# Block-diagonal attention tiles, division per query row, long loads, and attention merged into feed-forward in a fixed order

## The chip, the cores and the metric

One core of one Trainium2 chip runs the whole program. The metric is the device time of that core in microseconds (us); lower is better. Repeated runs of one kernel differ by up to some 1.5%.

## The reference

Sparse attention over 8 batches of 8 heads (576 positions, head size 64) is followed by a feed-forward network (FFN) on the 4608 resulting rows of 512 values. Four heads look only at the last 32 positions, four only at every 32nd position.

```python
rel = pos[:, None] - pos[None, :]
mask_local   = (rel >= 0) & (rel < 32)
mask_strided = (rel >= 0) & (pos[None, :] % 32 == pos[:, None] % 32)
# heads 0-3 local, 4-7 strided; softmax over the masked scores; times v
# x: [4608, 512], the heads side by side
h = x @ w_in                     # [512, 2048]
r = np.maximum(h, 0.0)
g = s * (r * r) + b              # s, b: one number each
return g @ w_out                 # [2048, 512]
```

## The kernel before

Attention is computed transposed: keys lie on partitions, queries run along the columns. AV, the product of the weights with V, also gives the sum of each query's weights, in row 64 of its PSUM tile. Since queries are columns, dividing by that sum means dividing by a row: the row is copied out for each head, one reciprocal per batch is taken over all of them, TensorE spreads it over 64 partitions by a product with ones, and VectorE multiplies.

```python
def emit_av(st):
    ...                                      # cut: the matmuls into ps_or[0:65, queries]
    nc.vector.tensor_single_scalar(          # L231: one row of 576 sums
        out=den8[b][prow:prow + 1, pcol:pcol + S],
        in_=ps_or[D:D + 1, :], scalar=0.0, op=ALU.add)
    nc.scalar.copy(out=xT[m][64 * e:64 * e + 64, b * S:(b + 1) * S], in_=ps_or[0:D, :])

def emit_norm_batch(b):
    nc.vector.reciprocal(out=rec8, in_=den8[b])            # L240
    for m in range(4):
        for e in range(2):
            ...                              # cut: two matmuls rec8 -> ps_nb (L249)
            nc.vector.tensor_tensor(out=sl, in0=ps_nb[rbase:rbase + 64, :],
                                    in1=sl, op=ALU.mult)   # L255
```

The order is attention and FFN in turn: each batch is a loop over four pairs of heads, and a whole FFN block (128 matmuls of 512 columns) is issued after the third pair.

```python
for b in range(B):
    nc.gpsimd.dma_start(out=qk_nat[:, :, 0:D], in_=qf)     # rows of 64 values
    ...                                      # cut: k and v the same way
    for m in range(4):
        ...                                  # cut: transposes, four ACT copies, scores,
                                             # exp, mask; AV of the previous head
        if m == 1 and b > 0:
            emit_norm_batch(b - 1)
        if m == 2:
            for T in moe_sched.get(b, []):
                emit_moe_block(T)            # 64 + 64 matmuls, nothing between them
```

The softmax here doesn't subtract the row's maximum and nothing guards it: scores larger than these inputs give would overflow.

## Time and profile before

| | before |
|---|---|
| time, median of 3 runs | 602.73 us (602.71 to 604.86) |
| span of the profiled run | 602.0 us |
| period of one batch and one FFN block | 65.1 us: FFN 27.3, attention 37.8 |
| mean granted clock in these two stretches | 0.96 and 0.62 |
| first FFN matmul | 97.3 us (the chain has its first at 98.7) |
| matmul columns of attention in a batch | 28.6 thousand |

The page's lines on engines, the chain and the stretches are in the prediction. One more view is needed, the groups of the division on VectorE (DVE). Columns: line, engine, operation, tiles, count, then busy us in all, mean ns of one, and the idle time before it with what ended most of that.

```profile
L231 DVE TENSOR_SCALAR den<-ps_or 1x576 f32<-1x576 f32 x64 | 48.2, 753 | 29.9 <-PE ps_or L222 29.2
L255 DVE TENSOR_TENSOR xT<-ps_nb,xT 64x576 f16<-64x576 f32 x64 | 48.3, 755 | 21.4 <-PE ps_nb L249 20.3
L240 DVE RECIPROCAL rec<-den 128x1152 f16<-128x1152 f32 x8 | 58.8, 7353 | 0.3
```

These are 155 us of DVE work for what is one division per query and head. A copy of one partition by 576 columns costs as much as a multiply of 64 partitions by 576: the length of the row counts, not the number of partitions.

### The profile page before, as it was taken

What the parts mean: (1) busy time and instruction counts of PE and PEld (TensorE: products, weight loads), DVE (VectorE), ACT (ScalarE), POOL (GpSimd) and SP (SyncE); (2) the same over time, 40 slices, a digit from 0 to 9 for tenths busy, and PEclk for the clock granted to TensorE, in tenths of its full rate; (3) what the DMA queues carried; (4) which work ended last, traced back from release to release, by engine and by line L of the source; (5) the groups of instructions that cost most, each with busy time, mean ns of one, the idle gap of its engine ahead of it and who ended that gap; (6) DMA issues with size and microseconds to landing.
All of it is one profiled execution on the core that took longest, in us unless ns stands there. A gap on an engine that the chain in (4) does not pass through costs nothing.

```text
span 602.0 us, 6889 instructions
## 1 busy us (share of the span) xinstructions
PE 507.0 (84%) x2576; PEld 238.9 (40%) x2576; DVE 322.4 (54%) x684; ACT 304.8 (51%) x579; POOL 45.7 (8%) x30
## 2 busy tenths in 40 slices
PE   0537889997999789987999799978998899939997
PEld 0313443444344434444344434443444444414443
DVE  1204686448742875268634874287536763485241
ACT  0538865437570857266543757085726664306050
POOL 5212111001200120010100120010000000000000
PEclk9996556995599658985699559965897569859999
DMA  9999949016901659015901690160000000100101
GB/s 114 202 175 77 65 27 78 14 58 40 78 2 56 54 31 49 36 42 33 79 16 55 40 77 3 66 45 1 2 35 36 0 2 17 53 0 2 52 18 70
DMA packets 119793, 28.59 MB, mean 47 GB/s; under 512 B 112208, under 2 KB 114640, under 8 KB 119760
## 3 DMA queue, kind: packets, MB, share of 16 engines
q0 software_dynamic: 113568, 18.35, 51.3%
q1 hardware_dynamic: 6192, 9.80, 4.4%
q8 instruction: 20, 0.33, 0.2%
q14 instruction: 13, 0.11, 0.1%
HBM read 37.06 MB, written 9.44 MB: 77 GB/s over the span
## 4 chain that ended last, share of the span: by engine, by line
PE 66%; DVE 15%; ACT 8%; DMA 5%; issue 4%; POOL 1%; ACTq 0%; POOLq 0%
PE ps_o L199 21%; PE ps_h L189 19%; PE ps_or L222 12%; DVE rec L240 10%; PE ps_s L316 7%; DMA w_out_sb<-in_moe_w_out_dram 5%; PE ps_nb L249 4%; DVE xT L255 3%; ACT pt L324 3%; DVE den L231 2%; ACT uT L194 2%; ACT xT L234 1%; PE ps_tq L285 1%; PE ps_tk L295 1%; DVE pt L330 1%
## 5 line engine op out<-in xcount | busy, mean ns | idle before, releaser
L324 ACT ACTIVATE pt<-ps_s 128x512 f16<-128x512 f32 (+4 forms) x240 | 97.8, 437 | 176.3 <-PE ps_s L316 131.2
L189 PE MATMUL ps_h<-xT,w_in_sb 128*128 128x512 f16 x576 | 140.6, 398 | 1.4 <-ACT uT L194 0.7
L199 PE MATMUL ps_o<-w_out_s,gT 128*128 128x512 f16 x576 | 125.8, 379 | 0.0
L194 ACT ACTIVATE uT<-ps_h 128x512 f16<-128x512 f32 x144 | 85.7, 597 | 69.5 <-PE ps_h L189 66.5
L222 PE MATMUL ps_or<-pt,v 128*65 128x64 f16 (+11 forms) x608 | 96.2, 276 | 22.1 <-DVE pt L330 12.6
L316 PE MATMUL ps_s<-qT,kT 64*128 64x159 f16 (+6 forms) x352 | 85.6, 339 | 24.3 <-ACT kT L301 16.3
L195 DVE TENSOR_TENSOR gT<-uT 128x512 f16<-128x512 f16 x144 | 61.3, 426 | 77.9 <-ACT uT L194 77.7
L189 PEld LDWEIGHTS <-w_in_sb 128*128 128x128 f16 x576 | 56.7, 101 | 75.7 <-issue 17.0
L222 PEld LDWEIGHTS <-v 128*65 128x65 f16 (+1 forms) x608 | 59.8, 140 | 59.9 <-issue 38.4
L199 PEld LDWEIGHTS <-gT 128*128 128x128 f16 x576 | 56.3, 98 | 68.0
L204 DVE TENSOR_TENSOR osb<-ps_o,bcs 128x512 f32<-128x512 f32 x36 | 24.9, 692 | 96.1 <-PE ps_o L199 96.1
L231 DVE TENSOR_SCALAR den<-ps_or 1x576 f32<-1x576 f32 x64 | 48.2, 753 | 29.9 <-PE ps_or L222 29.2
L255 DVE TENSOR_TENSOR xT<-ps_nb,xT 64x576 f16<-64x576 f32 x64 | 48.3, 755 | 21.4 <-PE ps_nb L249 20.3
L240 DVE RECIPROCAL rec<-den 128x1152 f16<-128x1152 f32 x8 | 58.8, 7353 | 0.3
L316 PEld LDWEIGHTS <-kT 64*128 64x128 f16 (+1 forms) x352 | 31.2, 115 | 64.2 <-issue 38.2
L330 DVE TENSOR_TENSOR pt<-pt,mask_str 128x512 f16<-128x512 f16 (+1 forms) x192 | 47.7, 303 | 5.1 <-ACT pt L324 3.3
L249 PE MATMUL ps_nb<-rec,hsel 128*64 128x512 f16 (+1 forms) x128 | 38.7, 438 | 13.6 <-DVE rec L240 8.3
L330 DVE TENSOR_TENSOR pt<-pt,mask_loc 128x159 f16<-128x159 f16 (+3 forms) x160 | 26.7, 222 | 40.5 <-ACT pt L324 39.5
L234 ACT CAST xT<-ps_or 64x576 f16<-64x576 f32 x64 | 40.2, 628 | 3.3 <-DVE den L231 2.4
L285 PE MATMUL ps_tq<-ident,qk_nat 128*128 128x128 f16 x128 | 20.6, 290 | 16.1 <-DMA qk_nat<-in_k_dram 16.1
L274 POOL DMA_DIRECT2D v<-in_v_dram x8 | 14.5, 1812 | 239.8 <-PE ps_or L222 232.6
L300 ACT COPY qT<-ps_tq 64x576 f16<-64x576 f16 x32 | 20.2, 631 | 14.9 <-PE ps_tq L288 14.9
(26 smaller groups left out, 188.1 us busy)
## 6 DMA issues: line engine op xcount, KB each, us to landing
out_dram<-osb SPq DMA_DIRECT2D x36, 256.0 KB, 2.0
qk_nat<-in_q_dram POOLq DMA_DIRECT2D x8, 576.0 KB, 9.2
qk_nat<-in_k_dram POOLq DMA_DIRECT2D x8, 576.0 KB, 10.5
v<-in_v_dram POOLq DMA_DIRECT2D x8, 576.0 KB, 8.5
w_in_sb<-in_moe_w_in_dram POOLq DMA_DIRECT2D x1, 2048.0 KB, 22.8
w_out_sb<-in_moe_w_out_dram POOLq DMA_DIRECT2D x1, 2048.0 KB, 27.1
mask_str<-mask_str SPq DMA_DIRECT2D x1, 160.0 KB, 2.5
hsel<-hsel SPq DMA_DIRECT2D x1, 64.0 KB, 1.9
```

The costliest lines, as they stand in the source:

```text
L189: nc.tensor.matmul(out=ps_h, lhsT=w_in_sb[:, ct, ft * 128:(ft + 1) * 128], rhs=xT[ct][:, tok0:tok0 + PS], start=(ct == 0), stop=(ct == 3))
L194: nc.scalar.activation(out=uT, in_=ps_h, func=AF.Relu)
L195: nc.vector.tensor_tensor(out=gT[:, ft, :], in0=uT, in1=uT, op=ALU.mult)
L199: nc.tensor.matmul(out=ps_o, lhsT=gT[:, ft, tsub * 128:(tsub + 1) * 128], rhs=w_out_s[:, ft, :], start=(ft == 0), stop=(ft == nftile - 1))
L222: nc.tensor.matmul(out=ps_or[0:D + 1, a:bq], lhsT=v1[rr, NT * m + t, 0:D + 1], rhs=pt[rr, p["c0"] + (a - p["i0"]): p["c0"] + (bq - p["i0"] ...
L231: nc.vector.tensor_single_scalar(out=den8[b][prow:prow + 1, pcol:pcol + S], in_=ps_or[D:D + 1, :], scalar=0.0, op=ALU.add)
L240: nc.vector.reciprocal(out=rec8, in_=den8[b])
L249: nc.tensor.matmul(out=ps_nb[rbase:rbase + 64, c0:c1], lhsT=hsel[:, 64 * (hh % 4):64 * (hh % 4) + 64], rhs=rec8[:, pcol + c0:pcol + c1], s ...
L255: nc.vector.tensor_tensor(out=sl, in0=ps_nb[rbase:rbase + 64, :], in1=sl, op=ALU.mult)
L316: nc.tensor.matmul(out=ps_s[poff:poff + nk, p["c0"]:p["c0"] + p["nq"]], lhsT=kT[rbase:rbase + 64, j0:j0 + nk], rhs=qT[rbase:rbase + 64, p[ ...
L324: nc.scalar.activation(out=pt[row_lo:row_hi, 0:W], in_=ps_s[row_lo:row_hi, 0:W], func=AF.Exp, scale=scale)
L330: nc.vector.tensor_tensor(out=pt[poff:poff + nk, p["c0"]:p["c0"] + p["nq"]], in0=pt[poff:poff + nk, p["c0"]:p["c0"] + p["nq"]], in1=masks[ ...
```

## The change

The intent was fourfold. Each mask becomes dense blocks: a local head is six tiles of 96 queries by 128 keys, a strided head, with its positions regrouped modulo 8, eight tiles of 72 by 72. AV puts queries on partitions, so that the division is a reciprocal of 4 or 6 columns and one multiply out of PSUM, and the result is transposed back. The loads of q and k take long pieces (6 or 8 positions of a head at once). And the attention of the next batch is dealt out between the matmuls of the current FFN block, in an order that the program fixes. The change is a rewrite; its core is below, with cuts. It also does something outside the four parts.

```diff
-        nc.gpsimd.dma_start(out=qk_nat[:, :, 0:D], in_=qf)
+            nc.gpsimd.dma_start(
+                out=tl, in_=src[b, 0:4].rearrange("h (p j) d -> p h (j d)", j=LT))
...
+                r0, at = (64 * e, j * nq) if loc else (64 * (j % 2), (4 * e + j // 2) * nq)
+                rr = slice(r0, r0 + 64)
+                nc.tensor.matmul(                              # L205, scores
+                    out=ps[0:nk, c:c + nq], lhsT=st["k"][rr, at:at + nk],
+                    rhs=st["q"][rr, at:at + nq])
...
+                    st["a"] = psum.tile([128, 6, D + 1], FP32, tag="a", bufs=1, name="ps_a")
+                nc.tensor.matmul(                              # L234, AV
+                    out=ps[0:nq, j % per, :],
+                    lhsT=st["pt", e, grp(j)[0]][0:nk, grp(j)[1], :],
+                    rhs=vt[0:nk, 2 * mm + e, j, :])
+                if j % per == per - 1:
+                    nc.vector.reciprocal(out=rec[0:nq, 0:per], in_=ps[0:nq, 0:per, D:D + 1])
+                    nc.vector.tensor_tensor(                   # L242
+                        out=st["x"][:, j0:j0 + per, 64 * e:64 * e + 64],
+                        in0=ps[0:nq, 0:per, 0:D],
+                        in1=rec[0:nq, 0:per].to_broadcast([nq, per, D]), op=ALU.mult)
...
+            # one phase of a batch: scores and transposes by halves, then AV, transposes of x
+            seq += Sn[:len(Sn) // 2] + Tn[:len(Tn) // 2] + Sn[len(Sn) // 2:] + Tn[len(Tn) // 2:]
...
-                for T in moe_sched.get(b, []):
-                    emit_moe_block(T)
+            for i, f in enumerate(seq):
+                at.setdefault(int(i * 112 / len(seq)), []).append(f)
+        for n, f in enumerate(F):                # F: the 128 FFN matmuls of block T
+            for g in at.get(n, []):
+                g()
+            f()
```

## The prediction

> **What bounds the kernel now.** I read the page first: shares of engines, then the slices, then the chain, then stretches of one period.
>
> ```profile
> PE 507.0 (84%) x2576; PEld 238.9 (40%) x2576; DVE 322.4 (54%) x684; ACT 304.8 (51%) x579; POOL 45.7 (8%) x30
> ...
> PE   0537889997999789987999799978998899939997
> ...
> PEclk9996556995599658985699559965897569859999
> ```
>
> PE looks busy everywhere, but the clock row swings between full and half. So PE is the bound in two ways. The chain of waits shows one period, here the third feed-forward (FFN) block and what follows it:
>
> ```profile
> 235.63 9.66 PE ps_h L189 x44
> 245.28 13.81 PE ps_o L199 x64
> 259.42 0.76 PE ps_or L222 x8
> 263.64 1.09 ACT pt L324 x2
> 265.89 0.94 PE ps_or L222 x7
> 266.86 0.77 DVE den L231
> 267.64 7.35 DVE rec L240
> 275.15 1.70 PE ps_or L222 x12
> ```
>
> 64 matmuls of 512 columns in 13.81 us are 216 ns each: the full clock, nothing to gain. After them the chain hops between PE, ACT and DVE and sits 7.35 us in one reciprocal. The stretches of that period (FFN, attention) say it in numbers:
>
> ```profile
> core 0: us, PE busy (x) PEld busy (x) DVE busy (x) ACT busy (x) POOL busy (x), PEclk, DMA share, GB/s
> ...
> 229.75:257.00 27.25, 27.20 (x122) 11.85 (x122) 9.73 (x21) 11.59 (x20) 0.00 (x0) 0.96 0.17 28
> 257.00:294.81 37.81, 31.36 (x185) 16.09 (x183) 29.11 (x62) 24.03 (x51) 5.43 (x3) 0.62 0.90 55
> ```
>
> A period is 65.1 us: 27.3 of FFN with DVE and ACT a third busy, and 37.8 of attention at a mean clock of 0.62, with DVE at 77%. The two engines that attention needs idle while FFN runs, and PE is slow while attention runs. The list of waits adds the start, where PE waits for data and then again for the weights:
>
> ```profile
> PE ps_tq L285 <- DMA qk_nat<-in_k_dram: 16.1, 1, 16.1
> ...
> PE bcs_ps L167 <- DMA w_out_sb<-in_moe_w_out_dram: 13.4, 1, 13.4
> ```
>
> The first FFN matmuls of the chain are at 98.7 us.
>
> **What the Trainium skill says.** (1) "TensorE: Matmul & The Clock Gate", Part 1: the array runs at half rate until a window of about 3.4 us has been busy, and falls back when it is not. The trace agrees: its clock record knows only full and half, in stretches of 30.7 and 34.1 us, nine and ten windows; windows in which matmul columns filled 38 to 45% of the full-rate cycles were followed by half clock, windows at 57% were not by themselves. (2) "TensorEngine Tiling (Array Packing)", Key Properties: changing the tiling mode drains the engine, and different row tiles run in parallel. The trace agrees on both. At full clock:
>
> ```profile
> 326.04 0.20 PE L288 MATMUL ps_tq<-ident,qk_nat 64*128 64x64 f16 x1
> 326.04 0.20 PE L291 MATMUL ps_tk<-ident,qk_nat 64*128 64x64 f16 x1
> 326.17 0.40 PE L295 MATMUL ps_tk<-ident,qk_nat 128*128 128x128 f16 x4
> 326.50 0.21 PE L316 MATMUL ps_s<-qT,kT 64*64 64x64 f16 x1
> 326.64 0.41 PE L222 MATMUL ps_or<-pt,v 128*65 128x512 f16 x1
> 326.98 0.40 PE L316 MATMUL ps_s<-qT,kT 64*64 64x512 f16 x1
> 327.31 0.35 PE L222 MATMUL ps_or<-pt,v 128*65 128x384 f16 x1
> ```
>
> L288 and L291 use opposite row halves and start together. A 512-column matmul of 128 rows followed by one of 64 rows takes 326.64 to 326.98, 0.34 us and not 0.216: a switch between 128 and 64 rows costs some 0.1 us; the 64-column one before it takes 0.14. (3) The same TensorE page, "Back-to-back issue gap", gives about 81 ns per matmul of 128 columns with its weight load. Here the measurement is lower: four L295 in 0.40 us, the last of which shows some 0.23, so 56 ns each; I use columns over 2.4 per ns. (4) "DMA: Bandwidth & Descriptors", Specifications: rows under 512 B miss line rate. The page counts 112208 of 119793 packets under 512 B, and DMA is above 90% in the first slices.
>
> **The change part by part.**
> Removed. Attention in 128-key tiles against wide query ranges is 28.6 thousand matmul columns a batch (4.6 transposes, 9.7 scores, 9.7 AV, 4.6 broadcast of the reciprocals). Block-diagonal tiles leave 15.2 thousand: 4.6 transposes, 4.6 scores, 3.6 AV (65 columns each, since V is now the moving operand) and 2.3 for transposing the result back. The DVE work on rows goes too: the reciprocal of 7.35 us, eight rows of denominators at 0.753 us and eight normalisations at 0.755 us, 19.4 us a batch.
>
> Added. Per batch 12 small reciprocals (4 or 6 columns; 7.35 us for 1152 columns is 6.4 ns a column, so about 0.15 us with the fixed part) and 12 multiplies out of PSUM, 256 or 384 columns. From 0.692 us at 512 and 0.755 at 576 columns I take 0.43 and 0.56. With the 16 squares (0.426), 16 masks (about 0.31), 4 output adds (0.692), copies and head pairing (about 3), DVE has some 25 us per merged block. ACT has 16 relus (0.597), 16 exponentials of 288 columns (0.41, between 0.386 at 256 and 0.570 at 477), 10 copies (0.63): 22.5 us.
>
> Moved. The order is fixed: seven FFN blocks are merged with the attention of the next batch, about 1.7 attention matmuls ahead of each FFN matmul; two FFN blocks stay alone. Reading the two programs' PE order, one merged block has 128 FFN matmuls, 196 of attention, and 72 switches between the 64-row scores and everything else. PE in one block, at full clock:
> - FFN 128 x 0.216 = 27.6 us.
> - Transposes and AV: 6.9 thousand columns / 2.4 = 2.9 us, and 56 x 0.034 = 1.9 us.
> - Scores: 56 in pairs on opposite row halves, 28 x 0.043 = 1.2 us.
> - Switches: 72 x 0.1 = 7.2 us.
> - Waits that the order leaves open. The AV bank has one buffer; it comes free after drain (0.2), reciprocal, multiply and two signals, about 0.9 us. Seven times a batch nothing but an FFN matmul stands between. Keys' copy before the scores: twice without cover, 1.2 us. I take 9 us less 2 for the FFN matmuls between: 7.
>
> Sum 47.8 us, in place of 65.1. PE stays the bound: DVE and ACT are about half busy, and the two-engine work lies beside FFN.
>
> Start. The loads of q and k now move rows of 768 B or more in 1344 pieces instead of 9216, two DMAs ahead of the first transposes. Issue is 0.78 us each from 1.3 us on (the time of the w_in issue, which has as few rows per partition); landing I estimate at 3.5 us after the second issue ends at 2.9 (the 256 KB stores land in 2.0, today's q loads of 4608 pieces in 7.4 after their issue), so 6.4, and the pairing of heads ends near 7 us, where the transposes waited until 16.1. Batch 0 then runs alone at half clock (four transposes there take 0.61 us, 107 ns each): 15.4 thousand columns / 1.2 = 12.8 us, and about 14 us of waits on ACT and DVE that nothing covers; 26.5. First FFN at 33.5 us, and w_in lands before that.
>
> Total: 33.5 + 7 x 47.8 = 368, + 16 x 0.216 for the bias product = 371.6, + 2 x 27.65 = 427, + 4 us from the last matmul to the end (598.0 to 602.0 now), + 0.7 between span and time (602.0, 602.7): 432 us.
>
> **The rivals.**
> The clock: if the merged stream falls back to half, a block takes 80.7 thousand columns / 1.2 = 67 us and more with switches and waits, and the kernel ends at 600 or above. Against it: the stream fills 80.7 / (47.8 x 2.4) = 70% of the full-rate cycles, well above the 38 to 45% that lost the clock. For it: FFN alone is 57%, the level seen once just before a fall; partial oscillation would give 450 to 480.
> Longer waits: DVE and ACT serve in order, so an AV eviction can stand behind a square, an output add or a mask. At 1.5 us for each of nine waits a block is 5 us longer: 467. For it speaks DVE at half of the block; against it, that most of those are 0.3 to 0.43 us.
> Switches cheaper than counted, where they coincide with a wait or the drain is hidden: 4 to 6 us off a block, about 395.
> 96 or 72 active rows counting as a mode of their own: then nearly every FFN matmul pays twice, and a block grows by 15 us or more: 540. No such shape is in this trace; 65 against 128 columns cost nothing in it.
> Transfers: V now takes 12 DMAs of 128 B rows per batch. At about 0.85 us of issue they need 10 us of POOL per block of 48; hidden, except perhaps at the start (up to 10 us).
>
> **Range and chances.** Waits and switches move the sum by 25 to 35 us either way, the clock only upward: 405 to 475. Faster by over 2% needs under 591; only a lasting half clock, or that and row modes together, breaks it: 0.97 faster, 0.02 same, 0.01 slower.
>
> **What would show it.** Clock near 1.0 from the first merged block to the end; first FFN matmul at 30 to 40 us; seven periods of 45 to 52 us; FFN matmuls in the last two blocks still 216 ns; PE's idle mostly ended by the multiply out of the AV bank and by key copies; scores' switches visible as gaps of 0.1 us. Wrong if periods are near 60 with clock 1.0 (waits, row modes), if the clock row shows fives after the first quarter, or if DMA ends PE's idle beyond the start.

## The result, and the profile after

The changed kernel takes 462.82 us (median of 4 runs, 459.20 to 465.23), the kernel before in the same rounds 603.80 (602.71 to 604.98). The ratio is 0.7665 with a 95% interval of 0.7623 to 0.7707. Ratios here are the mean time of one kernel's fast runs over that of the other's fast runs of the same rounds, so they are not quite the ratio of the medians quoted. The profiled run is the slowest of the four, 465.23 us.

The page's part 1, and from part 2 the rows of PE and of the granted clock:

```profile
PE 393.1 (85%) x2736; PEld 194.7 (42%) x2736; DVE 198.6 (43%) x557; ACT 177.7 (38%) x354; POOL 100.1 (22%) x137
...
PE   1848799788978989788978898888969797999995
...
PEclk9999999899999999899999999899999999899999
```

PE is busy for the same share as before, but the fives and sixes of the clock row are gone. DVE went from 322.4 to 198.6 us. (The nines at the very start are only the lack of a record: the transposes of 96 columns there start 80 ns apart, twice the 40 ns of the full clock.) The stretches of two merged blocks (us; busy time of PE, PEld, DVE, ACT and POOL with the number of instructions; clock; DMA share; GB/s), and one line of the chain for a block without attention:

```profile
198.53:249.05 50.52, 43.78 (x327) 21.66 (x326) 23.29 (x66) 20.74 (x42) 11.84 (x16) 1.00 0.45 59
249.05:300.80 51.75, 45.21 (x328) 22.21 (x327) 23.30 (x66) 20.73 (x42) 10.48 (x14) 0.97 0.43 57
```

```profile
403.13 13.81 PE ps_f L302 x64
```

A batch and an FFN block together now take 50.5 us at clock 1.00, or 51.75 with one window of half clock in them, in place of 65.1. Where no attention lies between, 64 FFN matmuls take the same 13.81 us as before.

What makes a merged block 50.5 us, where all its matmul columns at full rate are 33.6? The list of waits names the stops (us in total, times, longest):

```profile
PE ps_a L234 <- DVE x_nat L242: 42.0, 56, 1.6
...
PE ps_s L205 <- ACT kT_loc L180: 11.3, 16, 0.9
```

The first is the AV bank, seven times in each of the eight batches. The timeline shows one such stop (start, duration, engine, line, operation; in brackets the idle time before and what ended it):

```profile
233.57 0.19 PE L234 MATMUL ps_a<-v_str,pt 72*72 72x65 f16 x1
...
233.80 0.18 DVE L240 RECIPROCAL rec<-ps_a 72x4 f32<-72x4 f32 x1
...
234.02 0.42 DVE L242 TENSOR_TENSOR x_nat<-ps_a,rec 72x256 f16<-72x256 f32 x1
...
234.49 0.22 PE L234 MATMUL ps_a<-v_str,pt 72*72 72x65 f16 x1 [0.73 <-DVE x_nat L242]
```

The AV tile has one buffer. After its last matmul PE does nothing until the reciprocal (0.18 us) and the multiply (0.42 us) have read it. The FFN matmul of that place in the order stands behind the stopped AV matmul and starts only after it (at 234.55 us), so it does not fill the hole. The price of a switch between scores, which use 64 rows, and FFN matmuls, which use 128, is in the same timeline:

```profile
229.33 0.22 PE L205 MATMUL ps_s<-qTs,kTs 64*72 64x72 f16 x1
...
229.48 0.39 PE L317 MATMUL ps_f<-w_out_sb,gT 128*128 128x512 f16 x1
229.80 0.11 PEld L205 LDWEIGHTS <-kTs 64*72 64x72 f16 x2 [0.23 <-issue]
229.80 0.22 PE L205 MATMUL ps_s<-qTs,kTs 64*72 64x72 f16 x2
229.96 0.10 PEld L317 LDWEIGHTS <-gT 128*128 128x128 f16 x1
229.96 0.39 PE L317 MATMUL ps_f<-w_out_sb,gT 128*128 128x512 f16 x1
```

From start to start: 229.48 to 229.80, so an FFN matmul followed by a score takes 0.32 us in place of 0.216; and 229.33 to 229.48, so 72 columns take 0.15 in place of 0.03. Each direction costs about 0.11 us. (The durations in the second column are modelled ends and overlap; use the starts.) By contrast FFN matmuls next to transposes of 96 rows or AV of 72 rows start 0.22 us apart: those row counts cost nothing against 128.

```profile
235.39 0.38 PE L317 MATMUL ps_f<-w_out_sb,gT 128*128 128x512 f16 x1
...
235.61 0.21 PE L257 MATMUL ps_t<-ident,x_nat 96*128 96x96 f16 x1
```

The weight loads (PEld) show what a switch changes. At all 72 switches of the clean block below, a load starts at most 5 ns before its own matmul. Behind a 512-column matmul of like row mode it starts some 0.22 us before its own, so it lies under the matmul that runs. A load takes 0.10 to 0.11 us, about the price of a switch; so the price may be a load that is no longer hidden, or a drain of the array. The runs do not separate the two.

The times from start to start of all matmuls in the clean block of 198.5 to 249.05 us, each less its columns at full rate, add up so. The 72 switches are about 0.11 each, or 7.9 us. The nine stops, seven for the AV bank and two for the copies of the keys, are 8.0, some 0.9 each; the list of waits has 5.3 and 1.4 for them, because it counts from the modelled end of the matmul before. The other matmuls cost some 6 ns each beyond their columns, 1.4 us, and scores that follow a score win 0.4. With 33.6 us of columns that is the block.

### The profile page after: what moved, and what is told of

It is laid out like the page before. It is cut to its first block, busy times and chain, and to the rows that moved or that the text cites. A ratio compares the mean times of both kernels' runs of the same rounds, so it can differ in the third digit from the quotient of the medians.

```text
span 463.5 us, 6912 instructions
## 1 busy us (share of the span) xinstructions
PE 393.1 (85%) x2736; PEld 194.7 (42%) x2736; DVE 198.6 (43%) x557; ACT 177.7 (38%) x354; POOL 100.1 (22%) x137
## 4 chain that ended last, share of the span: by engine, by line
PE 71%; DVE 9%; ACT 7%; DMA 6%; issue 3%; POOL 2%; ACTq 0%; POOLq 0%
PE ps_f L302 27%; PE ps_f L317 26%; PE ps_s L205 9%; DVE x_nat L242 5%; PE ps_a L234 4%; ACT u L307 4%; DMA kl<-in_k_dram 3%; PE ps_t L169 3%; DMA qs<-in_q_dram 2%; ACT kT_loc L180 2%; DVE rec L240 2%; PE ps_t L257 1%; DVE o L322 1%; DVE gT L308 1%; ACT kTs L185 1%
## 5 line engine op out<-in xcount | busy, mean ns | idle before, releaser
L302 PE MATMUL ps_f<-xT,w_in_sb 128*128 128x512 f16 x576 | 178.2, 388 | 0.0
L317 PE MATMUL ps_f<-w_out_sb,gT 128*128 128x512 f16 x576 | 166.9, 393 | 0.0
L307 ACT ACTIVATE u<-ps_f 128x512 f16<-128x512 f32 x144 | 86.0, 597 | 72.9 <-PE ps_f L302 72.3
L308 DVE TENSOR_TENSOR gT<-u 128x512 f16<-128x512 f16 x144 | 61.3, 426 | 109.2 <-ACT u L307 109.2
L234 PEld LDWEIGHTS <-pt 72*72 72x72 f16 (+1 forms) x448 | 44.1, 127 | 71.3 <-DVE x_nat L242 58.3
L211 ACT ACTIVATE pt<-ps_s 72x288 f16<-72x288 f32 (+1 forms) x128 | 48.2, 407 | 59.8 <-PE ps_s L205 58.4
L234 PE MATMUL ps_a<-v_str,pt 72*72 72x65 f16 x256 | 39.1, 211 | 29.1 <-DVE x_nat L242 28.8
L242 DVE TENSOR_TENSOR x_nat<-ps_a,rec 72x256 f16<-72x256 f32 (+1 forms) x96 | 44.6, 465 | 3.3
L234 PE MATMUL ps_a<-v_loc,pt 128*96 128x65 f16 x192 | 27.3, 209 | 13.2 <-DVE x_nat L242 13.2
L205 PE MATMUL ps_s<-qTl,kT_loc 64*128 64x96 f16 x192 | 26.3, 221 | 11.3 <-ACT kT_loc L180 11.3
L205 PE MATMUL ps_s<-qTs,kTs 64*72 64x72 f16 x256 | 34.4, 222 | 0.8 <-ACT pt L211 0.5
L257 PE MATMUL ps_t<-ident,x_nat 72*128 72x72 f16 (+1 forms) x224 | 29.9, 215 | 0.5 <-DVE x_nat L242 0.5
```

Source lines behind the costliest of these rows:

```text
L205: nc.tensor.matmul(out=ps[0:nk, c:c + nq], lhsT=st["k"][rr, at:at + nk], rhs=st["q"][rr, at:at + nq])
L211: nc.scalar.activation(out=pt[0:nk].rearrange("k t c -> k (t c)"), in_=ps[0:nk, 0:half * nq], func=AF.Exp, scale=scale)
L234: nc.tensor.matmul(out=ps[0:nq, j % per, :], lhsT=st["pt", e, grp(j)[0]][0:nk, grp(j)[1], :], rhs=vt[0:nk, 2 * mm + e, j, :])
L242: nc.vector.tensor_tensor(out=st["x"][:, j0:j0 + per, 64 * e:64 * e + 64], in0=ps[0:nq, 0:per, 0:D], in1=rec[0:nq, 0:per].to_broadcast([nq ...
L257: nc.tensor.matmul(out=ps[:, nq * j:nq * j + nq], lhsT=st["x"][:, j, :], rhs=ident[0:nq, 0:nq], is_transpose=True)
L302: nc.tensor.matmul(out=st["h"], lhsT=w_in_sb[:, ct, ft * 128:(ft + 1) * 128], rhs=xT[ct][:, tok0:tok0 + PS], start=(ct == 0), stop=(ct == 3))
```

## The experiments

All had three rounds, and all compare with the kernel before run on the same chip. Its median was 602 to 604 us in every set, so medians of different sets can be set side by side.

**1. No change of row mode.** All scores use 128 rows, which computes wrong scores (two heads, or two groups of positions, are summed). The outputs still pass the comparison. It means that a pass says little about the scores; the later experiments that pass change only order and buffers.

```diff
-                rr = slice(r0, r0 + 64)
+                rr = slice(0, 128)
```

> Scores contract all 128 rows instead of one half of 64, so the result is wrong on purpose; PE never changes its row mode. Theory (a switch costs 0.1 us and 72 of them add up in each of seven merged blocks): a block loses some 8 us of gaps and gives back 0.7 us, because scores on opposite row halves no longer run together; about 50 us in all, 413 us, ratio to the changed kernel 0.89. Rival (the drains only take time that PE would spend waiting for VectorE or ScalarE anyway): under 20 us, 445 or more, with the waits for the multiply out of the AV bank grown by as much as the gaps shrank. In both the gap between an FFN matmul and a score falls from 0.32 to 0.22 us.

Measured: 414.94 us (414.04 to 418.83), ratio 0.6911. An FFN matmul followed by a score now starts the next after 0.216 us, a block without a clock fall takes 43.9 to 44.0 us, and the waits for the AV bank and the keys are as before (43.2 and 11.3 us). A clean block is 6.5 us shorter, 46 in seven. The clock also falls only twice in place of five times, so not all of the 48 us is the switches' own. The switches' cost comes in addition to the waits and is not hidden in them. The weight load of the matmul after a 512-column one starts some 0.22 us ahead again. Two lines of this run show a score between FFN matmuls without the hole:

```profile
202.17 0.20 PE L205 MATMUL ps_s<-qTs,kTs 128*72 128x72 f16 x1
202.20 0.38 PE L317 MATMUL ps_f<-w_out_sb,gT 128*128 128x512 f16 x1
```

**2. Two buffers for AV**, paid for with one of the three FFN banks.

```diff
-  st["a"] = psum.tile([128, 6, D + 1], FP32, tag="a", bufs=1, name="ps_a")
+  st["a"] = psum.tile([128, 6, D + 1], FP32, tag="a", bufs=2, name="ps_a")
-  ... tag="f", bufs=3 ...      # three places
+  ... tag="f", bufs=2 ...
```

> The AV accumulator gets two PSUM banks, the FFN accumulator two instead of three. Theory (the single AV bank stops PE seven times a batch, 0.75 us each, 42 us in all, and these stops also thin one 3.4 us window at the end of each batch's attention so that the clock falls): PE's waits for the multiply fall from 42 to under 10 us, the half-clock windows after the first FFN start vanish, about 425 us, ratio 0.92. Rival (FFN with two banks now waits for the relu as often): PE waits for the relu appear, 455 or more.

Measured: 413.92 us (413.61 to 414.30), ratio 0.6873. A block takes 44.46 us. The wait is all but gone:

```profile
PE ps_a L234 <- DVE x_nat L242: 2.6, 9, 0.6
```

That is 39.4 us of the gain of 49 (42 by the block times). The rest is the clock, which does not fall any more once it is full at 37.3 us, and an earlier first FFN matmul (34.0 us). My number, 425, left out the clock. The lost FFN bank cost only 0.14 us in an FFN block without attention (27.77 against 27.63).

**3. Not merged.** The same tiles, but the attention of the next batch is issued ahead of each FFN block instead of inside it.

```diff
-            for i, f in enumerate(seq):
-                at.setdefault(int(i * 112 / len(seq)), []).append(f)
-            for i, f in enumerate(last):
-                at.setdefault(118 + int(i * 3 / len(last)), []).append(f)
+            at[0] = seq + last
```

> All attention of the next batch stands ahead of the FFN block instead of between its matmuls; tiles, loads and division as in the changed kernel. Theory (block-diagonal tiles bring most of the gain, merging hides only the waits): attention alone takes about what batch 0 takes, 25 to 28 us, mostly at half clock, a period is 54 us, 480 to 495 us in all, ratio 1.05. Rival 1 (merging brings most of the gain): periods return towards the 65 us of the kernel before, 540 or more. Rival 2 (merging brings nothing): 463 within 2%.

Measured: 484.12 us (483.34 to 486.40), ratio 0.8045. The clock row swings again as in the kernel before:

```profile
PEclk9999999965899569965899559965899559999999
```

After a first one of 57.2, a period is 54.1 to 54.6 us, 23.9 of them at half clock. So of the 141 us that the change gained, 120 came without the merge: the tiles, the division, the loads and the moved scaling of w_out. The first FFN matmul is at 62.5 us in place of 97.3, six periods are about 10.3 us shorter on the mean, and some 23 us fall to the end of the program. Merging, the part meant to keep the clock up, brought 21 us. Switches and AV stops took most of what the clock gave: without most of them the merged form gains another 87 us (experiment 6). Bundled scores and a second bank without the merge were not run.

**4. Short loads.** q and k are fetched in pieces of 128 or 256 B, one transfer per head, all else as changed.

```diff
-            nc.gpsimd.dma_start(
-                out=tl, in_=src[b, 0:4].rearrange("h (p j) d -> p h (j d)", j=LT))
+            for h in range(4):
+                nc.gpsimd.dma_start(
+                    out=tl[:, h, :, 0:D], in_=src[b, h].rearrange("(p j) d -> p j d", j=LT))
```

> q and k land in rows of 128 B (local heads) and 256 B (strided heads) with one DMA per head, so the long loads are undone; V and weights as in the changed kernel. Theory (loads matter only at the start): the first transpose comes 3 to 8 us later, the periods stay at 50 to 52 us, 466 to 472 us. Rival (descriptors and POOL's issue become a bound in every block): PE waits for DMA or for the pairing of heads in every block, 490 or more.

Measured: 467.63 us (463.57 to 469.59), ratio 0.7756. The first FFN matmul comes at 38.1 in place of 35.2 us, and clean merged blocks are unchanged, 50.5. The long loads are worth some 5 us, all at the start; that is less than the 6 us by which runs of one kernel differ, so the size is rough. The expected delay of the first transpose did not come (6.1 us, against 6.7): before the first FFN matmul PE waits for V instead (3.2 us), and in the first block for w_out (2.6). Later the transfers are hidden in either form. (The edit also pads the tiles in SBUF, so that the pieces stay apart.)

**5. Scores issued together.** The scores of half a phase follow each other without an FFN matmul between: 16 switches a block instead of 72; the arithmetic is unchanged.

```diff
+    def one(steps):
+        def f():
+            for g in steps:
+                g()
+        return [f] if steps else []
-            seq += Sn[:len(Sn) // 2] + Tn[:len(Tn) // 2] + Sn[len(Sn) // 2:] + Tn[len(Tn) // 2:]
+            seq += one(Sn[:len(Sn) // 2]) + Tn[:len(Tn) // 2]
+            seq += one(Sn[len(Sn) // 2:]) + Tn[len(Tn) // 2:]
```

> The six or eight scores of each half phase stand together instead of being spread between FFN matmuls; nothing else changes, and the result is right. Switches of the row mode per merged block fall from 72 to 16. Theory (0.11 us a switch, adding up): 56 x 0.11 = 6 us a block, and all scores now run in pairs, 0.5 us more; 45 us in all, about 416 us, ratio to the changed kernel 0.90. Rival (spreading the scores was what covered their waits): the waits for exponentials and key copies grow and take back half, 440.

Measured: 408.38 us (407.01 to 409.03), ratio 0.6767. A block takes 43.53 us and the clock never falls after it is full. The AV waits shrank too (33.2 us), and the waits for key copies grew (16.1). It is 8 us below the expected 416, which left the AV stops and the clock as they were. Against experiment 1, where no switch is left at all, a block is 0.5 us shorter: its 16 switches cost 1.6, but scores next to each other win 0.5 and the stops are 1.4 less. With two clock falls of 1.2 us gone and a first FFN matmul 1.1 us earlier, that is about the lead of 6.5.

**6. Experiments 2 and 5 together.**

> Scores together, and two PSUM banks for AV with two for FFN. Theory (switches and AV stops are separate costs that add): both gains, some 45 and 50 us, 368 us. Rival (they cover each other, one gap is filled by the other's stop): 390 or more. The clock stays at full from the first FFN matmuls on.

Measured: 375.72 us (374.73 to 377.51), ratio 0.6223, the clock full from 41.2 us on, a block 38.48 us. The two gains add up but for 1.0 us a block. In the whole, 16 us are missing (48.9 and 54.4 alone, 87.1 together), some 6 of them because each alone had already removed the same five clock falls; so it lies 8 us above the expected 368. The 16.0 us of waits for the key copies are now the largest left.

**7. Room for the key copy.** To 6, six empty places are added behind phases 0 and 1 and between the halves of phase 4, so that FFN matmuls lie between a copy and its scores; and in the first block attention starts 16 FFN matmuls later.

```diff
+            gap = [lambda: None] * 6
+            if ph == 4:
+                seq += one(Sn[:len(Sn) // 2]) + gap + one(Sn[len(Sn) // 2:])
...
+            if ph < 2:
+                seq += gap
...
-                at.setdefault(int(i * 112 / len(seq)), []).append(f)
+                n0 = 16 if T == 0 else 0
+                at.setdefault(n0 + int(i * (112 - n0) / len(seq)), []).append(f)
```

> As the last, and FFN matmuls are kept between the last key transposes and the scores that wait for the key copy (six empty places in the order after the first two phases and between the last two halves of scores), and in the first merged block the attention starts 16 FFN matmuls later, so that FFN does not wait for the next batch's q. Theory: PE's waits for key copies (11 us) go, and 3 us at the start of the first block, 355 us. Rival: the waits move to exponentials or to the relu with only two FFN banks, 366 or more.

Measured: 363.01 us (361.20 to 363.60), ratio 0.6012. The key wait fell to 1.5 us and a block to 35.98. I missed by 8 us, for a reason in the list of waits:

```profile
PE ps_f L354 <- DMA w_out_sb<-in_moe_w_out_dram: 10.0, 1, 10.0
```

The first block now needs w_out before it has arrived. PE stands from 50.6 to 60.6 us, and the clock falls to half from 55.4 to 65.6.

**8. w_out loaded earlier.** To 7, the load of w_out is issued ahead of the V of batch 1.

```diff
-    load_v(1)
     load_w_out()
+    load_v(1)
```

> As the run with all three edits, with w_out loaded ahead of V of batch 1. Theory: PE's wait of 10 us for w_out in the first block goes and with it the fall of the clock there, 350 to 356 us. Rival: V of batch 1 then comes too late and PE waits for it instead, 361 or more.

Measured: 357.33 us (356.93 to 358.43), ratio 0.5930 [0.5907, 0.5952]; the outputs pass. This is the fastest version, and it beats both kernels. The wait for w_out is gone, a smaller one for V (3.5 us) has come, which is why it just missed the expected 350 to 356. The clock still falls, from 49.0 to 55.9 us, after a window in which PE waited 2.8 us for V; the expectation had that fall gone. Its page:

```profile
PE 331.9 (93%) x2736; PEld 177.5 (50%) x2736; DVE 194.6 (55%) x557; ACT 168.8 (48%) x354; POOL 100.6 (28%) x137
```

Its blocks of 35.98 us stand against 33.6 us of columns: no stop is left in a block, and 16 switches are 1.6 of the 2.4 us between.

**9. The kernel before without its division.** Sums, reciprocal, spreading and multiply are left out of the kernel before (wrong, relative error 1.99), to see whether that chain alone was its bound.

```diff
-        nc.vector.tensor_single_scalar(          # den8, the rows of sums
-            ...
-            if m == 1 and b > 0:
-                emit_norm_batch(b - 1)
...
-    emit_norm_batch(B - 1)
```

> The kernel before without its normalisation: no denominator rows, no reciprocal, no broadcast matmuls, no multiplies over the rows; the result is wrong on purpose. This is the division part of the change alone, at no cost. Theory A (attention in the kernel before was held up by VectorE and the chain through it, 77% busy): 19.4 us of VectorE a batch go, periods fall from 65 to about 52 us, some 490 to 510 us. Theory B (attention was bound by matmul columns at half clock): only the 4.6 thousand broadcast columns count, 3.8 us a batch, 570 us.

Measured: 537.33 us (536.08 to 537.86), ratio 0.8916. The gain of 66 us, 8.3 a batch, lies between the two expectations: neither "the division is the bound" nor "it hides beside other work" holds. DVE is only 31% busy, yet the clock still falls to half in every attention stretch:

```profile
PEclk9998555997589956996599658995699569979999
```

The chain shows what is left there, one round of hops and the start of the next:

```profile
420.50 0.51 ACT xT L227
421.01 0.55 ACT qT L293
421.57 0.65 ACT kT L294
...
422.26 0.71 PE ps_s L309 x4
...
426.59 0.51 ACT xT L227
```

Three copies in a row on ACT, 1.7 of the 6.1 us of a round, lie on the path between one pair of heads and the next.

## Why the prediction was right or wrong

The range of 405 to 475 held the 462.8 us. The centre, 432, was 31 us low, and 33 below the profiled run of 465.23, from which the steps are read. Step by step:

- **The bound.** Right. PE stays the bound; DVE and ACT do 23.3 and 20.7 us in a merged block, where the prediction had 25 and 22.5.
- **The start.** Nearly right: the first FFN matmul is at 35.2 us against 33.5 (the 15.4 thousand columns there are 15.2 by the prediction's own count, a slip of 0.2 us). The first transpose is at 6.7 us ("near 7" was said), but only that of the queries; the keys landed later, and PE waited another 2.6 us for them.
- **The merged block, 47.8 us.** Here lies the miss. Clean blocks take 50.5, blocks with a clock fall 51.6 to 52.0, and the first takes 59.6, of which 3.45 are the bias product that was counted apart. Six blocks at a mean of 51.3 are 21 us over, the first 8 us over; with 1.7 at the start that is 31 us. The other 2 lie behind the last matmul: 5.2 us to the end of the span where 4 were said, and 1.8 between span and time where 0.7 were.
- **Which terms.** The mechanism was right, the terms were each a little small. Switches: 7.2 predicted, 7.9 measured, because each costs 0.11 and not 0.1. Waits: 7 predicted, 8.0 measured. The prediction credited 2 us for FFN matmuls that would fill the stops; they could not, since they stand behind the stopped matmul. Scores: counted wholly as pairs running together, but only 20 of the 56 of a block stand next to another; the others pay for their columns one by one, which makes 1.6 us in place of 1.2. All other matmuls cost 1.4 us beyond their columns, where the prediction had 0.7. These sum to about 2.7 us in a clean block.
- **The clock.** The prediction wanted it near 1.0 "from the first merged block to the end", and let it fail only as a lasting half rate or as an oscillation worth 450 to 480. Two smaller things happened. The first 9.6 us of the first merged block ran at half rate, which is 4.8 us, after batch 0 alone, whose windows the columns had filled to at most 73% even of the half rate. And five of the seven merged blocks lost one window of 3.4 us, 1.2 us each against the clean ones. Each fall followed a window at the end of an attention phase in which matmul columns filled 38 to 40% of the full rate's cycles. The prediction had set the mean filling of a block (70%; measured, 67%) against levels of single windows; the single windows of a merged block run from 38 to 98%. Its reading of the trace before was too narrow as well: falls there follow windows of 22 to 50%, not only of 38 to 45. The total landed in the oscillation rival's interval, but the clock explains only some 11 of the 31 us, so that rival is not what happened.
- **96 or 72 rows as a mode of their own.** Refuted, as the prediction leaned: next to 128 rows they start without a gap.
- **Longer waits.** The rival with 1.5 us each is refuted as a mean: the 42.0 us over 56 stops are 0.75 each, and only the longest is 1.6 (as the list counts; from start to start the mean is 0.9, which the prediction had).
- **Transfers.** Right: hidden after the start. Experiment 4 shows that even the short form would have been, after the first block.

The experiments confirm the two disputed terms. The prediction's sum holds 7 blocks by 7.2 us, or 50, for switches; removing them gave 46 in the blocks and 48 in all (experiment 1), and all but 16 of 72 in a block gave 54, smaller AV waits and the steady clock included (experiment 5). It holds 7 by 7, or 49, for waits; a second AV bank gave 49 (experiment 2), but that the two agree is luck: 39 of these were the waits for the AV bank, the rest clock and start, while the waits for keys, which the 49 of the prediction include, stayed. What the prediction did not see is that both are properties of the order and of one buffer, so that they could be removed. The Trainium skill, "PSUM — Partial Sum Buffer", section "PSUM bank collisions raise a hardware error", says that two engines may not be in one bank and quadrant at once. So, as long as the next AV tile lies in the same bank, its matmul has to wait; the trace agrees (it starts 0.05 us after the multiply's end). A second bank removes the stop; more FFN matmuls before the next tile should hide it too (not tried for AV). Here it costs 0.75 us on the mean, as the list counts, and the page names no price.

As to where the 141 us came from: 120 need no merge (experiment 3); some 5 are the long loads (4); the old division alone, at no cost in its place, is worth 66 in the old kernel (9). How these 66 would split between the reciprocal and the rows of sums was not measured, nor was the gain of the narrower tiles by themselves.

## What to carry to other kernels

When work is merged into a dense stream on an engine that works in the order of the program, as PE does here, every stop of the merged part stops the dense part as well; so give the merged part a second buffer, put dense work between a producer and its user, and keep matmuls of unlike row counts in bundles. Count the changes of row mode and the single-buffered evictions in the order before running it: here 72 and 7 per block, at 0.11 and 0.75 us, were 87 of the 463 us, the clock falls that went with them included, when nearly all the AV stops and 56 of the 72 switches were taken out (experiment 6). Once those are gone, look at the loads again, because a faster start meets the next transfer (experiment 7).

## What the Trainium skill lacked or had wrong

- "TensorEngine Tiling (Array Packing)", Key Properties, says that a change of mode drains the engine, but not what it costs, nor which mode 72 or 96 active rows belong to. Here it is about 0.11 us in each direction between 64 and 128 rows, with a weight load of 0.10 us that starts only with its own matmul, and nothing between 72, 96 and 128.
- "TensorE: Matmul & The Clock Gate", Part 1, gives the window and the two rates, and as a rule that no idle gap be longer than a window; it adds that frequent short idling makes the clock swing too, but gives no level of filling. Here the clock fell with no single wait of PE over 1.6 us in the merged blocks: in this kernel and in experiments 1, 2 and 5 after all seven full-clock windows that columns filled to 38 to 40%, and after none of the 32 at 42 to 51%. (Columns are counted over the time in which they stream; the windows follow the clock record.) No level holds for both kernels: the kernel before lost the clock after five of six windows at 42 to 50%. What decides it stays open.
- The same page, "Back-to-back issue gap", has about 81 ns for a matmul of 128 columns in a real stream, and 131 for 512. This case has 56 and 216 at full clock in the kernel before, and 29 to 33 ns for 65 columns in the merged stream, each with its own weights loaded. Part 1 of the page, with 55.6 and 215.7 ns, fits.
- No page puts a price on a PSUM tile with one buffer in a merged stream: 0.75 us a stop, 42.0 us in all.
